# Attention with two expert networks on one core: the network's square and affine step on ScalarE, the second group's solve on VectorE alone, and a new order of the work between the attention hops

## The chip, the cores and the metric

The kernel runs on one core of one Trainium2 chip. The metric is the time of one execution on the device in microseconds. TensorE multiplies matrices (its weight loads are listed as PEld), VectorE (DVE), ScalarE (ACT) and GpSimd (POOL) work on tiles of 128 partitions, SyncE (SP) starts transfers. Each engine runs its own instructions in order; between engines there are semaphores.

## The reference

```python
def _attn_ref(q, k, v, beta):
    k_n = k / (np.linalg.norm(k, axis=-1, keepdims=True) + 1e-06)
    for t in range(S):
        y[:, :, t] = np.einsum('bhd,bhde->bhe', q[:, :, t], state)
        v_old = np.einsum('bhde,bhd->bhe', state, kt)
        state = state + bt[:, :, :, None] * np.einsum('bhd,bhe->bhde', kt, vt - v_old)

def _moe_ref(x, w_in, w_out, s, b):
    h = x @ w_in
    r = np.maximum(h, 0.0)
    g = s * (r * r) + b
    return (g @ w_out).astype(np.float32)

def reference(**kwargs):
    attn_out = _attn_ref(**attn_kwargs)
    x = attn_out.transpose(0, 2, 1, 3).reshape(B * S, H * D)
    x = _moe_ref(x=x, **moe_kwargs)
    return _moe2_ref(x=x, **moe2_kwargs)
```

Four batches of eight heads, 768 steps, 48 wide, feed 3072 tokens of 384 to a network of 2048 hidden units; `_moe2_ref` sends each token through the best of eight experts of 1024 hidden units. All is fp32.

## The kernel before

**Attention.** The sequence is cut into 24 chunks of 32 steps, and these into six groups of four. Within a chunk the update is a triangular system of 32 x 32 per head. For a whole group it is solved at once: `lanes_in` transposes the Gram matrices `gc` so that every partition holds one system A, prepares T, the norms and the scaling of A, and scales v by the norms on POOL; `solve` takes 31 steps of two VectorE instructions (`tmp` = column of A times row of T, T minus `tmp`); `lanes_out` transposes T into `tt`. Then `dstep` runs a chunk in three hops: `ks` (state times keys, X = v minus it), `tx` (T times X, giving `u` and `bdu`), `ku` and `mu` (new state `ds`, `sst`; output). Each hop hands on from TensorE to VectorE and back. The hops of a group are the fixed chain; group 0 runs alone, and the others take the next group's preparation with them: loads, `tr_k`, `tr_q`, `gram`, `lanes_in`, the solve steps, `lanes_out`, each with a due time in hops (`add`, `due`).

**Second group.** It has no hops to hide behind. `lanes_in(1)`, 15 steps `solve_d` on the two diagonal halves of every system, and the off-diagonal quarter by products: `off_in`, then four times `off_1` (TensorE, copy by ScalarE) and `off_2` (TensorE, update of `tt` by VectorE). `PREP` says how many ticks of network work follow each piece.

**First network.** `moe1` is a generator; each tick it emits one fp32 matmul (first token pair, `kk` = 0) or three matmuls of the split form (later pairs: high and low part of x and of the weights). Twelve pairs of 256 tokens, eight blocks each: `mm1` fills the one PSUM buffer `h`, Relu frees it; then square, scale by s and add b, cast to the high part `gh`, difference `gl`; `mm2` two blocks later uses both. In the first pair ScalarE does square and affine step; in later pairs POOL does (L698, L699). Calls put into `later` come a given number of ticks on.

**Order.** The order on TensorE, VectorE, ScalarE and POOL is the order of emission. In the hops of group g, `run_moe` emits at each of 48 quarter hops as many ticks as are left to a target, 192 g - 36, divided by the quarter hops left. Every fifth tick calls `w_next`: first `x_step` (weight words are put together: two VectorE instructions and a sum on POOL, L580), then `split_step` (cast by ScalarE, difference by VectorE into `wp`). After the last hop the rest of the network runs alone, then the second network.

## Time and profile before

| | |
|---|---|
| median of 3 runs | 991.92 us (991.78 to 992.33) |
| profiled execution | 991.13 us, span 989.1 us |
| TensorE busy | 879.0 us (89%), 12602 matmuls |
| weight loads busy | 799.1 us (81%) |
| VectorE busy | 477.5 us (48%), 1009 instructions |
| ScalarE busy | 331.9 us (34%), 689 |
| POOL busy | 251.8 us (25%), 262 |
| mean granted TensorE clock | 0.924 of full speed |

A busy TensorE is not one at its peak: the clock is granted at one of two levels, 1.2 and 2.4 GHz, and 0.92 is a mean over both. The share of busy time is a mean over stages: group 0 alone (to about 86 us), the preparation of the second group (to 174), the hops of groups 1 to 5 (to about 653), the rest of the first network (to about 740), the second network. In the rows, times are microseconds from the start of the span unless marked ns; what stands in brackets is the idle time ahead of an instruction and what ended it.

### The profile page before, as it was taken

Reading aid. Unit: us, or ns where it says so; the run is one execution under the profiler, and the core shown is the slowest. Engines: PE = TensorE matmul, PEld = TensorE weight load, DVE = VectorE, ACT = ScalarE, POOL = GpSimd, SP = SyncE. Lnnn points to the kernel's source line nnn. Section 1 sums busy time; section 2 is a strip of 40 time slices with the busy share of each in tenths; the row PEclk is TensorE's granted clock in tenths of the full one; section 3 lists DMA queues with packets and bytes.
Section 4 is the critical chain, followed back from the end, with each engine's and each line's share of the span. In section 5 each row is a group of like instructions: output and inputs, shape, how many; then the busy total and the mean of one; then the engine's idle time right before and its main releaser. Section 6 shows DMA issues by size and latency. Waiting matters only on the chain. (4 is left out here: it accounts for less than half of the span.)

```text
span 989.1 us, 28725 instructions
## 1 busy us (share of the span) xinstructions
PE 879.0 (89%) x12602; PEld 799.1 (81%) x12602; DVE 477.5 (48%) x1009; ACT 331.9 (34%) x689; POOL 251.8 (25%) x262
## 2 busy tenths in 40 slices
PE   6288779975997999989998999999997999999997
PEld 4266567865997999888997999999996779779796
DVE  3975595549534973489327942226314333231111
ACT  2515644431342334323342332335322222222221
POOL 4122340112223332143323333334430110110100
PEclk7658987887999999999998999999998999999999
DMA  8762132011220121102100000005008310123000
GB/s 153 248 229 52 32 53 48 19 35 18 46 47 11 31 48 27 31 19 49 34 3 2 18 3 18 18 2 176 17 1 52 49 49 25 56 84 124 17 33 25
DMA packets 115597, 49.48 MB, mean 50 GB/s; under 512 B 89943, under 2 KB 112144, under 8 KB 115472
## 3 DMA queue, kind: packets, MB, share of 16 engines
q1 hardware_dynamic: 108560, 46.44, 20.2%
q10 hardware_dynamic: 6336, 1.18, 0.8%
q8 instruction: 99, 1.62, 0.7%
q14 instruction: 26, 0.21, 0.1%
q0 software_dynamic: 576, 0.02, 0.1%
HBM read 38.06 MB, written 9.74 MB: 48 GB/s over the span
## 5 line engine op out<-in xcount | busy, mean ns | idle before, releaser
L698 POOL TENSOR_TENSOR r<-r 128x512 f32<-128x512 f32 x88 | 96.1, 1092 | 356.9 <-ACT r L697 356.9
L724 PE MATMUL acc<-gh,wp 128*128 128x256 f32 x1056 | 146.2, 284 | 0.0
L677 PE MATMUL h<-xh,wp 128*128 128x256 f32 x576 | 124.5, 298 | 11.7 <-ACT r L697 11.7
L724 PEld LDWEIGHTS acc<-gh,wp 128*128 128x128 f32 x1056 | 133.7, 193 | 1.2
L701 DVE TENSOR_TENSOR gl<-r,gh 128x512 fp32r<-128x512 f32 x88 | 63.0, 716 | 128.6 <-ACT gh L700 128.5
L677 PEld LDWEIGHTS h<-xh,wp 128*128 128x128 f32 x576 | 98.3, 198 | 14.3 <-ACT r L697 12.7
L700 ACT CAST gh<-r 128x512 fp32r<-128x512 f32 x88 | 54.7, 622 | 149.5 <-POOL r L699 139.2
L677 PE MATMUL h<-xhl,wp 128*128 128x256 f32 x720 | 101.5, 288 | 3.3 <-ACT r L697 3.3
L965 DVE SCALAR_TENSOR_TENSOR hl<-h,hh 128x512 fp32r<-128x512 f32 x46 | 31.7, 691 | 141.5 <-ACT hh L964 141.5
L677 PEld LDWEIGHTS h<-xhl,wp 128*128 128x128 f32 x720 | 90.0, 190 | 5.3 <-ACT r L697 3.9
L697 ACT ACTIVATE r<-h 128x512 f32<-128x512 f32 x88 | 52.6, 598 | 93.3 <-PE h L677 64.2
L677 PE MATMUL h<-xl,wp 128*128 128x256 f32 x288 | 83.0, 288 | 0.0
L699 POOL TENSOR_SCALAR r<-r,s_sb,b_sb 128x512 f32<-128x512 f32 x88 | 74.9, 851 | 9.2
L724 PE MATMUL acc<-gl,wp 128*128 128x256 f32 x528 | 75.8, 279 | 0.0
L425 ACT COPY x<-ch 32x384 f32<-32x384 f32 x96 | 45.2, 471 | 87.3 <-PE ch L411 86.3
L287 DVE TENSOR_TENSOR T<-T,tmp 128x31 f32<-128x31 f32 (+15 forms) x155 | 69.4, 448 | 5.3
L724 PEld LDWEIGHTS acc<-gl,wp 128*128 128x128 f32 x528 | 67.4, 190 | 0.2
L284 DVE TENSOR_TENSOR tmp<-A,T 128x31 f32<-128x31 f32 (+15 forms) x155 | 65.1, 420 | 3.9
L1045 PE MATMUL o<-w2h,hh 128*128 128x384 f32 x184 | 62.3, 339 | 0.0
L1045 PE MATMUL o<-w2l,hh 128*128 128x384 f32 x184 | 61.9, 336 | 0.0
L1045 PE MATMUL o<-w2h,hl 128*128 128x384 f32 x184 | 61.8, 336 | 0.0
L1034 POOL TENSOR_TENSOR x2l<-xr,x2h 128x512 fp32r<-128x512 f32 x15 | 18.7, 1279 | 166.3 <-ACT x2h L1033 166.3
(226 smaller groups left out, 1493.9 us busy)
## 6 DMA issues: line engine op xcount, KB each, us to landing
wr<-in_moe_w_in SPq DMA_DIRECT2D x16, 384.0 KB
wr<-in_moe_w_out SPq DMA_DIRECT2D x8, 768.0 KB
v<-in_v SPq DMA_DIRECT2D x192, 24.0 KB
x2d<-x2s SPq DMA_DIRECT2D x24, 192.0 KB
out<-o SPq DMA_DIRECT2D x24, 192.0 KB
kpad<-in_k SPq DMA_DIRECT2D x160, 24.0 KB
qpad<-in_q SPq DMA_DIRECT2D x40, 96.0 KB
xr<-x2d SPq DMA_DIRECT2D x5, 768.0 KB
```

The lines of the kernel that those rows point to most:

```text
L284: nc.vector.tensor_tensor(out=tmp, in0=A[:, j + 1:, j:j + 1].to_broadcast([128, m, j + 1]), in1=T[:, j:j + 1, 0:j + 1].to_broadcast([128, ...
L287: nc.vector.tensor_tensor(out=T[:, j + 1:, 0:j + 1], in0=T[:, j + 1:, 0:j + 1], in1=tmp, op=ALU.subtract)
L425: nc.scalar.copy(out=x_t[gi][pb:pb + C, :, r * 96:(r + 1) * 96].rearrange("p h (g e) -> p h g e", g=2), in_=y[32 * rr:32 * rr + 32, :, :, ...
L677: nc.tensor.matmul(out=h[:, f, :], lhsT=wi_(w, 2 * j + f, m), rhs=x[:, m, :], start=(m == 0 and i == 0), stop=(m == KD - 1 and i == 2))
L697: nc.scalar.activation(out=r, in_=h, func=AF.Relu)
L698: nc.gpsimd.tensor_tensor(out=t, in0=r, in1=r, op=ALU.mult)
L699: nc.gpsimd.tensor_scalar(out=t, in0=t, scalar1=s_sb, scalar2=b_sb, op0=ALU.mult, op1=ALU.add)
L700: later.append((step[0] + 7, lambda: nc.scalar.copy(out=gh, in_=t)))
L701: later.append((step[0] + 9, lambda: nc.vector.tensor_tensor(out=gl, in0=t, in1=gh.bitcast(F32), op=ALU.subtract)))
L724: nc.tensor.matmul(out=acc[:, m * TT:(m + 1) * TT], lhsT=wo_(w, 2 * j + f, m * 128, 128) if kk else wx_(2 * j + 1, 2 * j + f, m * 128), rh ...
L965: nc.vector.scalar_tensor_tensor(out=hl, in0=ps, scalar=0.0, in1=hh.bitcast(F32), op0=ALU.max, op1=ALU.subtract)
L1045: nc.tensor.matmul(out=ps, lhsT=h[:, sl], rhs=w[:, f, :], start=(f == 0 and i == 0), stop=(f == KF2 - 1 and i == 2))
```

## The change

The later pairs' square and affine step go to ScalarE, as in the first pair: Square directly after Relu, the affine step and the cast seven ticks on, `gl` eleven ticks on instead of nine. POOL keeps the weight sums of `x_step`, group 0's v-scaling and the second network's part.

`lanes_in` is cut into `lanes_1`, `lanes_2`, `lanes_3` and two calls of `scale_v`, each an item with a due time of its own, half a hop to one hop ahead of the solve. The clearing of T and, from the second group on, the scaling of v are VectorE's.

The second group is solved like the others, 31 steps on VectorE; `diag`, `solve_d`, `off_in`, `off_1` and `off_2` are gone. `PREP` and the due times of the items are new, and weight step, router and lanes alternate differently.

In the hops, the quarter hops from the 24th on count double in group 1 and one and a half times later when the ticks left are shared out; up to eight ticks may follow a quarter hop. One weight scaling fewer is emitted ahead of the first solve.

```diff
-    def lanes_in(gi):
...
+    def lanes_1(gi):
+        A = stg.tile([128, C, C], F32, tag="A", name="A")
         nc.vector.transpose(out=A, in_=gc_t[gi].rearrange("p h g n t -> p t (h g n)"))
...
+        T = T0.pop() if gi == 0 else stg.tile([128, C, C], F32, tag="gc", name="T")
         if gi:
-            nc.gpsimd.memset(Tf, 0.0)
+            nc.vector.memset(T, 0.0)
...
+    def scale_v(gi, g, eng):
+        if g == 0:
+            nmc_t[gi] = stg.tile([128, C], F32, tag="ss", name="nmc")
+            nc.vector.transpose(out=nmc_t[gi], in_=ln[gi][2])
+        nv = nmc_t[gi].rearrange("p (h g n) -> p h n g", g=2, h=B)
+        o = v_t[gi][:, :, :, g, :]
+        eng.tensor_tensor(
+            out=o, in0=o, in1=nv[:, :, :, g].unsqueeze(3).to_broadcast([128, B, HG, D]), op=ALU.mult)
...
-    PREP = {1: 2, 2: 12, 3: 3, 4: 10, 5: 1}
+    PREP = {100: 2, 200: 5, 201: 4, 300: 2, 301: 1, 400: 5}
...
                 if gi:
-                    h += 0.5
-                    add(h, lanes_in, g2)
-                    h += 0.5
+                    for f, a in ((lanes_1, ()), (lanes_2, ()), (lanes_3, ()), (scale_v, (0, nc.vector)),
+                                 (scale_v, (1, nc.vector))):
+                        add(h, f, g2, *a)
+                        h += 0.25
                     he = 11.25
                     for j in range(C - 1):
-                        add(h + max(0, he - h) * j / (C - 1), solve, g2, j)
+                        add(h + (he - h) * j / (C - 1), solve, g2, j)
                     add(he + 0.25, lanes_out, g2)
                 else:
-                    add(102, router_setup_a2)
-                    add(103, router_setup_b)
-                    add(200, lanes_in, 1)
-                    for j in range(C2 - 1):
-                        add(300 + j, solve_d, 1, j)
-                    add(400, off_in, 1)
-                    for n in range(HG):
-                        add(500 + 2 * n, off_1, 1, n, n + 1)
-                        add(501 + 2 * n, off_2, 1, n, n + 1)
-            items.sort(key=lambda x: x[:2])
+                    add(100, router_setup_a2)
+                    add(200, lanes_1, 1)
+                    add(200, lanes_2, 1)
+                    add(200, lanes_3, 1)
+                    add(201, scale_v, 1, 0, nc.vector)
+                    add(201, scale_v, 1, 1, nc.vector)
+                    add(201, router_setup_b)
+                    for j in range(C - 1):
+                        add(301 if j % 3 == 2 else 300, solve, 1, j)
+                    add(400, lanes_out, 1)
+            items.sort(key=lambda x: (min(x[0], 300) if x[0] > 100 else x[0], x[1]))
...
-                        st["gi"], st["left"] = gi, 4 * (NS - hops) - i
+                        st["gi"], n = gi, 4 * hops + i
+                        w = [(2 if gi == 1 else 1.5) if x >= 23 else 1 for x in range(n, 4 * NS)]
+                        st["left"] = sum(w) / w[0]
...
-            nc.scalar.activation(out=r, in_=h, func=AF.Relu)
-            nc.gpsimd.tensor_tensor(out=t, in0=r, in1=r, op=ALU.mult)
-            nc.gpsimd.tensor_scalar(out=t, in0=t, scalar1=s_sb, scalar2=b_sb, op0=ALU.mult, op1=ALU.add)
-            later.append((step[0] + 7, lambda: nc.scalar.copy(out=gh, in_=t)))
-            later.append((step[0] + 9, lambda: nc.vector.tensor_tensor(
-                out=gl, in0=t, in1=gh.bitcast(F32), op=ALU.subtract)))
+                def parts():
+                    nc.scalar.activation(out=r, in_=r, func=AF.Identity, scale=s_sb, bias=b_sb)
+                    nc.scalar.copy(out=gh, in_=r)
+                later.append((step[0] + 7, parts))
+                later.append((step[0] + 11, lambda: nc.vector.tensor_tensor(
+                    out=gl, in0=r, in1=gh.bitcast(F32), op=ALU.subtract)))
...
-        w_scale(7)
+        w_scale(6)
...
-                run_moe(max(1, min(7, -(-(24 * KF // 2 * st["gi"] - 36 - state["n"]) // st["left"]))))
+                run_moe(max(1, min(8, round((24 * KF // 2 * st["gi"] - 36 - state["n"]) / st["left"] + 0.3))))
```

What the order becomes at three places follows; line numbers are those of each program.

TensorE at the end of the second group's preparation, before (`z` are the off-diagonal products, `acc` the network's second layer, `ch` the first product of group 1's first hop):

```order
L326 MATMUL z_2195<-tt,gc 32x16 x32
L724 MATMUL acc<-gf,wr_262 128x256
L339 MATMUL z_2231<-zz,dd 32x16 x32
L724 MATMUL acc<-gf,wr_262 128x256
L355 MATMUL ch<-sst,kqt 64x48 x32
```

TensorE at the same place, now (`h` is the network's first layer, `u` the second hop's product):

```order
L633 MATMUL h<-xh,wp_1843 128x256
L307 MATMUL ch<-sst,kqt 64x48 x32
L678 MATMUL acc<-gf,wr_264 128x256 x4
L328 MATMUL u<-X,tt 32x48 x32
L678 MATMUL acc<-gf,wr_264 128x256 x2
```

The products `z` between network pieces are gone; whole blocks of the network stand ahead of group 1's first hop, and the second hop follows after four matmuls.

VectorE in the second group's lanes, before (`wr` are the weight steps, `tmp` and T the half solve):

```order
L266 TENSOR_TENSOR A<-A,bt 128x1024
L272 STREAM_TRANSPOSE nmc<-nm 128x32
L577 SCALAR_TENSOR_TENSOR wr_257<-wr_257 128x768
L579 TENSOR_SCALAR wr_257<-wr_257 128x768
L577 SCALAR_TENSOR_TENSOR wr_260<-wr_260 128x768
L579 TENSOR_SCALAR wr_260<-wr_260 128x768
L304 TENSOR_TENSOR tmp<-A,T 128x30
L307 TENSOR_TENSOR T<-T,tmp 128x2x15
```

VectorE at the same place, now:

```order
L268 TENSOR_TENSOR A<-A,bt 128x1024
L533 SCALAR_TENSOR_TENSOR wr_260<-wr_260 128x768
L535 TENSOR_SCALAR wr_260<-wr_260 128x768
L276 STREAM_TRANSPOSE nmc<-nm 128x32
L279 TENSOR_TENSOR v<-v,nmc 128x16x48
L533 SCALAR_TENSOR_TENSOR wr_262<-wr_262 128x768
L535 TENSOR_SCALAR wr_262<-wr_262 128x768
L279 TENSOR_TENSOR v<-v,nmc 128x16x48
```

The weight steps have moved in between the lane pieces, and the two scalings of v stand in VectorE's row.

ScalarE around the lanes of group 3's hops, before (`r` from `h` is Relu, `gh` the cast, `ss` the norms):

```order
L700 CAST gh<-r 128x512
L254 ACTIVATE s_4475<-ss 128x32
L697 ACTIVATE r<-h 128x512
```

ScalarE at the same place, now:

```order
L653 CAST gh<-r 128x512
L252 ACTIVATE s_4158<-ss 128x32
L641 ACTIVATE r<-h 128x512
L642 ACTIVATE r<-r 128x512
L652 ACTIVATE r<-r,b_sb,s_sb 128x512
```

Square and affine step of each block stand between its Relu and its cast.

## Rows read from the trace of the kernel before

**Rows 1.** Windows: span, busy PE, PEld, DVE, ACT, POOL; clock, DMA, GB/s

```profile
core 0: us, PE busy (x) PEld busy (x) DVE busy (x) ACT busy (x) POOL busy (x), PEclk, DMA share, GB/s
86.30:174.50 88.20, 70.17 (x1011) 57.27 (x1011) 55.16 (x98) 47.99 (x88) 22.76 (x15) 0.83 0.24 41
174.50:253.40 78.90, 62.12 (x1383) 55.79 (x1382) 52.54 (x116) 25.75 (x61) 13.95 (x13) 0.82 0.13 26
253.40:569.30 315.90, 296.60 (x5395) 283.56 (x5394) 192.31 (x402) 109.84 (x250) 103.97 (x105) 0.98 0.14 28
569.30:740.00 170.70, 169.74 (x2180) 166.56 (x2180) 57.71 (x103) 63.60 (x127) 66.31 (x69) 1.00 0.12 34
```

**Rows 2.** TensorE's waits, 253.4 to 569.3 us: total us, times, longest

```profile
PE h L677 <- ACT r L697: 15.1, 8, 3.9
```

**Rows 3.** Timeline, 421 to 427 us (group 3): start, us, instruction, [idle before]

```profile
421.11 2.91 POOL L276 TENSOR_TENSOR v<-v,nmc 128x768 f32<-128x768 f32 x2 [4.03 <-DVE nmc L272]
421.17 1.54 PE L724 MATMUL acc<-gh,wp 128*128 128x256 f32 x12
421.18 1.48 DVE L287 TENSOR_TENSOR T<-T,tmp 128x31 f32<-128x31 f32 x1
...
423.98 1.04 POOL L698 TENSOR_TENSOR r<-r 128x512 f32<-128x512 f32 x1
...
425.93 0.62 ACT L700 CAST gh<-r 128x512 fp32r<-128x512 f32 x1 [8.07 <-POOL r L699]
426.45 0.59 ACT L697 ACTIVATE r<-h 128x512 f32<-128x512 f32 x1
426.58 0.69 DVE L701 TENSOR_TENSOR gl<-r,gh 128x512 fp32r<-128x512 f32 x1 [3.92 <-ACT gh L700]
...
427.09 0.39 PE L677 MATMUL h<-xh,wp 128*128 128x256 f32 x1 [3.71 <-ACT r L697]
```

**Rows 4.** Windows of L287 alone (T minus tmp): first solve, group 3

```profile
26.70:52.50 25.80, 11.81 (x31) 0.61 0.81 269
359.20:464.90 105.70, 15.11 (x31) 0.98 0.17 33
```

**Rows 5.** Windows of L284 alone (tmp): the same two stretches

```profile
26.70:52.50 25.80, 11.77 (x31) 0.61 0.81 269
359.20:464.90 105.70, 13.83 (x31) 0.98 0.17 33
```

**Rows 6.** TensorE's waits, 174.5 to 253.4 us (group 1)

```profile
PE ds L392 <- DVE bdu L381: 11.1, 2, 6.3
```

**Rows 7.** Timeline of the preparation of the second group

```profile
116.53 0.47 DVE L815 TENSOR_SCALAR x2s<-x2s,ei 8x384 f32<-8x384 f32 x1
...
119.16 1.98 DVE L246 STREAM_TRANSPOSE A<-gc 128x1024 f32<-128x1024 f32 x1
...
154.40 2.01 DVE L314 STREAM_TRANSPOSE tt<-T 128x1024 f32<-128x1024 f32 x1
...
173.50 0.35 DVE L343 SCALAR_TENSOR_TENSOR tt<-z,negm,tt 128x128 f32<-128x128 f32 x1 [3.92 <-PE z L339]
...
176.59 1.02 DVE L361 TENSOR_TENSOR X<-v,ch 128x384 f32<-128x384 f32 x2 [1.88 <-issue]
...
180.91 0.88 PE L376 MATMUL u<-X,tt 32*32 32x48 f32 x64
```

**Rows 8.** Instruction groups: count, busy us, mean ns; the memset from the timeline

```profile
L688 ACT ACTIVATE r<-r 128x512 f32<-128x512 f32 x8 | 5.1, 632 | 0.3
L689 ACT ACTIVATE gf<-r,b_sb,s_sb 128x512 f32<-128x512 f32 x8 | 6.6, 824 | 1.5 <-PE acc L724 1.5
L590 DVE TENSOR_TENSOR wp<-wr,wp 128x768 fp32r<-128x768 f32 x11 | 10.6, 967 | 5.5 <-ACT wp L589 5.5
L307 DVE TENSOR_TENSOR T<-T,tmp 128x30 f32<-128x30 f32 (+7 forms) x15 | 7.5, 502 | 0.5
L304 DVE TENSOR_TENSOR tmp<-A,T 128x30 f32<-128x30 f32 (+7 forms) x15 | 3.8, 251 | 0.2
1.20 0.27 DVE L89 MEMSET qpad<- 128x256 f32 x1
```

More of the change, by code (lines that the diff above doesn't have):

```diff
@@ L267, in lanes_in @@
             out=A, in0=A, in1=bt.unsqueeze(2).to_broadcast([128, C, C]), op=ALU.mult)
-        ln[gi] = (Af, Tf)
-        def scale_v():
-            nmc = stg.tile([128, C], F32, tag="ss", name="nmc")
-            nc.vector.transpose(out=nmc, in_=nm)
-            nv = nmc.rearrange("p (h g n) -> p h n g", g=2, h=B)
-            for g in range(2):
-                o = v_t[gi][:, :, :, g, :]
-                nc.gpsimd.tensor_tensor(
-                    out=o, in0=o, in1=nv[:, :, :, g].unsqueeze(3).to_broadcast([128, B, HG, D]), op=ALU.mult)
-        scale_v()
+    nmc_t = {}
+    def scale_v(gi, g, eng):
[6 more added lines that the diff above has]
+            out=o, in0=o, in1=nv[:, :, :, g].unsqueeze(3).to_broadcast([128, B, HG, D]), op=ALU.mult)
     def solve(gi, j):
-        A, T = ln[gi]
+        A, T, _ = ln[gi]
         m = C - 1 - j
@@ L290, in lanes_out @@
     def lanes_out(gi):
-        A, T = ln.pop(gi)
-        tt_t[gi] = att.tile([128, 2 * HG * B, C], F32, tag="tt", name="tt", bufs=2)
+        A, T, _ = ln.pop(gi)
+        if gi not in tt_t:
+            tt_t[gi] = att.tile([128, 2 * HG * B, C], F32, tag="tt", name="tt", bufs=2)
         nc.vector.transpose(out=tt_t[gi].rearrange("p u t -> p t u"), in_=T)
-    def diag(x):
-        return x.rearrange("p t i -> p (t i)").rearrange("p (b x) -> p b x", b=2)[:, :, 0:C2 * C].rearrange(
-            "p b (t i) -> p b t i", i=C)[:, :, :, 0:C2]
@@ L310, in tile_kernel @@
-    of = {}
-    def off_in(gi):
-        A, T = ln.pop(gi)
-        nc.vector.transpose(out=tt_t[gi].rearrange("p u t -> p t u"), in_=T[:, 0:C])
-        dd = stg.tile([128, C + 1, C], F32, tag="A", name="dd")
-        nc.vector.transpose(out=dd[:, 0:C].rearrange("p u i -> p i u"), in_=T[:, 0:C].rearrange("p t i -> p i t"))
-        of[gi] = dd
-    def off_1(gi, n0, n1):
-        gc = gc_t[gi].rearrange("p h g n t -> p (h g n) t")
-        z1 = ps_pp.tile([128, 2 * B, n1 - n0, C2], F32, tag="pp", name="z1")
-        for n in range(n0, n1):
-            for e in range(2 * B):
-                for r in range(4):
-                    sl = slice(32 * r, 32 * r + 32)
-                    nc.tensor.matmul(out=z1[sl, e, n - n0, :], lhsT=gc[sl, e * HG + n, :],
-                                     rhs=tt_t[gi][sl, e * HG + n, C2:], start=True, stop=True)
-        zz = stg.tile([128, 2 * B, n1 - n0, C2], F32, tag="tmp", name="zz")
-        nc.scalar.copy(out=zz, in_=z1)
-        of[gi, n0] = zz
@@ L332, in off_2 @@
-    def off_2(gi, n0, n1):
-        dd, zz = of[gi], of.pop((gi, n0))
-        z2 = ps_pp.tile([128, 2 * B, n1 - n0, C2], F32, tag="pp", name="z2")
-        for n in range(n0, n1):
-            for e in range(2 * B):
-                for r in range(4):
-                    sl = slice(32 * r, 32 * r + 32)
-                    nc.tensor.matmul(out=z2[sl, e, n - n0, :], lhsT=dd[sl, e * HG + n, :], rhs=zz[sl, e, n - n0, :],
-                                     start=True, stop=True)
-        for n in range(n0, n1):
-            t = tt_t[gi].rearrange("p (e n) t -> p e n t", e=2 * B)[:, :, n, C2:]
-            nc.vector.scalar_tensor_tensor(out=t, in0=z2[:, :, n - n0, :], scalar=negm, in1=t,
-                                           op0=ALU.mult, op1=ALU.add)
@@ L530, in attention @@
                 if it[0] >= 100:
[L531 removed]
+                    yield PREP[it[0]]
         st["hop"] += 100
@@ L890, in tile_kernel @@
                         nc.scalar.copy(out=o, in_=i)
-        lanes_in(0)
+        lanes_1(0)
+        lanes_2(0)
+        lanes_3(0)
+        scale_v(0, 0, nc.gpsimd)
+        scale_v(0, 1, nc.gpsimd)
         cg = ps_c.tile([128, 2, HG * B, C], F32, tag="ch", name="gr")
```

44 lines of the change are left out of this document (14 added, 30 removed).

## The prediction

> **What bounds the kernel now.** I read the stretches first [rows 1]. From 569 to 740 us TensorE is busy 169.74 of 170.70 us: nothing but its own work counts there, and the change takes no matrix work out of it; the second network behind it has the same code. Time can come only from the three stretches ahead, where TensorE stands idle: the preparation of the second group (88.20 - 70.17 = 18.0 us idle, clock 0.83, so partly on the lower of its two levels), the hops of group 1 (78.90 - 62.12 = 16.8 us, 0.82) and the hops of groups 2 to 4 (315.90 - 296.60 = 19.3 us, 0.98).
>
> Then what the idle time waits for. In groups 2 to 4 it is one thing: 15.1 of the 19.3 us are eight waits of the network's first matmul of a block for the Relu that frees the only buffer `h` [rows 2]. The timeline shows one of them [rows 3]: POOL starts the two v-scalings at 421.11 and holds them to 424.02; only then come the square (1.04 us) and the affine step of the block before; ScalarE, which works in order, has stood 8.07 us at the cast of that block's `gh`, and the Relu of the next block, long possible, runs behind it at 426.45; TensorE starts at 427.09, 3.71 us late.
>
> POOL also slows VectorE. A solve instruction on 31 elements took 1.48 us while POOL ran [rows 3]; all 62 of the first solve take 11.81 + 11.77 = 23.6 us, those of the solve in group 3 take 15.11 + 13.83 = 28.9 [rows 4, 5]. So 5.4 us a group are stalls, at the least.
>
> In group 1 TensorE waits for VectorE's own queue: 11.1 us before the state products `ds` [rows 6]. In the preparation the half solve ends early (its result is transposed at 154.40) but the off-diagonal halves go round TensorE, ScalarE and VectorE until 173.50, each round waiting (3.92 us in the last); the first `u` of group 1 comes at 180.91 [rows 7].
>
> **The change part by part.**
>
> *Square and affine step to ScalarE.* In the 88 blocks after the first pass (11 token pairs of 8) POOL's two steps are replaced by a Square of 0.63 and an Identity of 0.82 us, prices that the first pass shows for the same tiles [rows 8]. ScalarE gets 1.45 us a block: 16 blocks a group, 23 us on top of 109.84 / 3 = 36.6 [rows 1], 60 of 105 us. It no longer waits for POOL, so the standstill of up to 8.07 us ahead of a Relu has no cause left. I take the 15.1 us of Relu waits as gone; the ends are 0 (all replaced by a longer queue) and 19.3 (all idle time gone). What then comes last in the late hops is VectorE.
>
> The Trainium skill speaks against this place: "ScalarE: Activation LUTs", section Rules for kernel authors, wants multiplications and additions on VectorE, not on ScalarE. Here the rows decide against the rule: VectorE, not ScalarE, is what the hops wait for; by the rule 32 more instructions a group, at the 0.69 us of a `gl` 22 us, would stand in its queue, and the sum would lose the gain of groups 2 to 4. I follow the rows.
>
> *Scaling v and clearing T on VectorE.* Per later group two instructions on 768 elements, 0.97 us each by the weight split of the same width, and a memset, 4 x 0.27 = 1.1 us by the one on 256 elements [rows 8]: 3.0 us more. Against it the 5.4 us of stalls go. Net on VectorE between -2.4 and +3.0 us a group; I take -1, since these 5.4 us have a row and the 3.0 are sure.
>
> *More network work in late hops.* Counted in the emitted order, a hop of groups 2 to 4 had 16 ticks (one tick is three matmuls) throughout; now it has 12 to 15 in the first six hops and 17 to 20 in the last six. By 1.54 us for 12 matmuls [rows 3] a tick is 0.35 to 0.39 us: four ticks cover 1.5 us more of a late hop. The sum over a group is the same 192 ticks, so TensorE's work is unchanged. But a late hop now has about 8 us of work on TensorE (20 ticks and an attention step like `u`, 0.88) and 8 on VectorE (31 solve steps over 4.25 hops, some 0.75 us each without stalls, one product of 1.0, one or two `gl` of 0.69): matched, not covered. I charge 2 us over the three groups for hops in which VectorE is late.
>
> **Groups 2 to 4: -15 + 2 = -13 us** (ends -22, which adds the time lost to the lower clock level, and -2).
>
> *Group 1.* In its first six hops the order had 8, 8, 8, 5, 4, 4 ticks and now has 4, 4, 4, 4, 4, 5: 12 fewer, and TensorE is nearly full there (11.1 of the stretch's 16.8 idle us are two waits of the last six hops [rows 6]), so 12 x 0.35 = -4 us. They were done in the preparation (102 ticks instead of 95) or come in the last six hops, which VectorE bounds, so that they cost nothing there as long as VectorE's queue is the longer one: those 11.1 us are their cover. With VectorE's own net of -1: **-5 us** (ends -8 and 0).
>
> *Preparation, second group on VectorE alone.* By differences of VectorE's queue up to the transpose at 154.40 [rows 7]. Added: the full solve 23.6 less the half one 7.5 + 3.8 = 11.3 [rows 4, 5, 8] is +12.3; v-scaling and memset +3.0; four more weight splits stand ahead of the transpose in the order, 4 x 0.97 = +3.9. Taken out: the lanes no longer wait for the router's transposes. They began at 119.16, the router's chain ends at 117.0 [rows 7], but the weight step that lay between is only moved behind them: -0.5. The transpose begins at 154.4 + 12.3 + 3.0 + 3.9 - 0.5 = 173.1. Behind it: transpose 2.0, a split 0.97, a `gl` 0.69 [rows 3], X 1.0, so `u` at 177.8 instead of 180.91. The 256 small matmuls, four copies and four updates of the off-diagonal path disappear; they were in nobody's way but their own. The weight sums on POOL remain and now fall between the lane pieces, where each may stall VectorE once: up to five stalls of at most 1.3 us (1.48 less the 0.19 of a free instruction). Against this the two POOL scalings and their stalls go. Ends: -8 and +5; I take **-3 us**, with the stalls of both sides even. Here is the change's weak point: VectorE becomes the only bound of the preparation, and ScalarE's casts of the splits, which wait for VectorE, stand in front of the Relus.
>
> *The rest.* One weight scaling fewer ahead of the first solve lies on ScalarE while it waits for data: 0. The network after the hops and the second network: 0, TensorE is full or the code is the same.
>
> Sum: -3 - 5 - 13 = -21 us. The profiled execution took 991.13 us (its span 989.1 and 2.0 around it), which gives 970; it lies 0.8 us under the median of 991.92, which gives **971**.
>
> **The rivals.**
> *Late hops stay bound by VectorE.* The Relu waits go, but the hop's chain X, `bdu`, `ds` waits in VectorE's queue as in group 1. For it: work is only matched. Against it: VectorE is busy 192.31 of 315.90 us there [rows 1]. Then groups 2 to 4 give 4 us: 991.9 - 3 - 5 - 4 = 980.
> *The preparation becomes longer.* ScalarE's casts wait for VectorE's splits and the Relus behind them, so all three engines move at the slowest, with stalls from POOL and TensorE at its lower clock after each pause. `u` 5 us later than before instead of 3 earlier: 971 + 8 = 979.
> *Everything idle in groups 2 to 4 goes*, and the preparation has no stalls: -22 - 8 - 5 = -35, 957.
> *Slower: ScalarE becomes the bound.* In order, it now holds Relu, Square, Identity and cast, 0.60 + 0.63 + 0.82 + 0.62 = 2.67 us a block, besides output and key copies. There is one buffer `h`, so a late Relu stops TensorE. It decides from 21 / 88 = 0.24 us a block on; at 0.5 us: 971 + 44 = 1015. Against it: 18 matmuls, over 2 us, lie between two first layers, and the cast alone held ScalarE for longer before.
> *It doesn't do what it says*: the weights of the late hops change little because the count is rounded. The order shows 20 instead of 16 ticks, so this is out.
>
> **How the numbers follow.** Forecast 971 (within 7 us): 0.50; VectorE-bound late hops 0.17; longer preparation 0.12; everything gone 0.13; slower 0.05; several shortfalls together that leave nothing 0.03. The range leaves out the slower cases and half of the best one: 958 to 984. A measurement of this kernel tells 0.2%, 2 us, from no change. Faster 0.92, same 0.03, slower 0.05.
>
> **What would show it.** Right: no wait of a cast for POOL; TensorE's Relu waits under 4 us in groups 2 to 4 and a group at about 101 us instead of 105.3; solve sums near 22 us; first `u` of group 1 at about 178, the first of group 2 some 8 us earlier than now. Wrong: Relu waits of 0.3 us at many blocks; new waits of `ds` or `u` for VectorE in groups 2 to 4; the first `u` of group 1 after 181.

## The result, and the profile after

The changed kernel takes 954.74 us in the median of its runs against 992.12 us of the kernel before on the same chip, a ratio of 0.9616 (95% interval 0.9598 to 0.9635). The forecast was 971 us, its range 958 to 984: the direction was right, the gain is 37 us instead of 21, and the time lies 3 us below the range. The profiled execution has a span of 953.3 us against 989.1, 35.8 us less.

Where the 35.8 us come from is read in windows between the first `u` products of the groups, which cut both kernels at the same place in the program. Of before, then of after (columns: start and end, length, busy us of PE, PEld, DVE, ACT, POOL with instructions, granted clock, DMA share, GB/s):

```profile
86.30:180.90 94.60, 76.57 (x1097) 63.08 (x1097) 58.04 (x102) 49.77 (x91) 22.76 (x15) 0.82 0.22 38
180.90:260.25 79.35, 62.57 (x1406) 56.65 (x1405) 54.37 (x118) 25.55 (x62) 16.25 (x15) 0.85 0.15 29
260.25:576.00 315.75, 296.45 (x5391) 283.42 (x5390) 192.31 (x400) 109.66 (x250) 104.96 (x105) 0.98 0.14 27
576.00:649.73 73.73, 73.73 (x1248) 71.46 (x1247) 22.24 (x42) 24.86 (x48) 23.62 (x26) 1.00 0.05 13
```

```profile
86.30:173.30 87.00, 62.69 (x591) 52.45 (x591) 66.37 (x131) 50.96 (x90) 15.59 (x9) 0.91 0.23 40
173.30:246.39 73.09, 61.98 (x1386) 55.97 (x1386) 52.61 (x122) 31.98 (x70) 0.00 (x0) 0.81 0.16 31
246.39:538.29 291.90, 288.60 (x5392) 277.44 (x5391) 174.51 (x409) 179.23 (x346) 0.00 (x0) 1.00 0.15 29
538.29:613.01 74.72, 74.72 (x1256) 72.44 (x1256) 22.13 (x42) 43.98 (x75) 0.00 (x0) 1.00 0.05 13
```

The preparation gives 7.6 us, group 1 6.3, groups 2 to 4 23.9; group 5 takes 1.0 us more and what follows 0.9 more. In groups 2 to 4 two things went: TensorE's idle time, 315.75 - 296.45 = 19.3 us, is 3.3; and the same matmuls are busy for 288.60 us instead of 296.45, since the granted clock is 1.00 of full speed throughout instead of 0.98.

TensorE's waits in groups 2 to 4 of after (total us, times, longest) answer to [rows 2]; what is left has nothing to do with Relu:

```profile
PE gr L220 <- issue: 2.2, 4, 0.8
PE acc L678 <- issue: 1.0, 1, 1.0
```

ScalarE at the lanes of group 2 in after, from the timeline (start, us, instruction, [idle before]), answers to [rows 3]. In these rows Square, affine step and cast follow Relu without a wait, and Relu waits for TensorE's matmul instead of the other way round. Over groups 2 to 4, 29 Relus wait for TensorE (55.1 us); three still wait for VectorE's `gl` (8.9 us, at most 3.0), without keeping TensorE waiting:

```profile
288.06 0.23 ACT L252 ACTIVATE s<-ss 128x32 f32<-128x32 f32 x1 [2.31 <-DVE ss L246]
289.65 0.60 ACT L641 ACTIVATE r<-h 128x512 f32<-128x512 f32 x1 [1.36 <-PE h L633]
290.28 0.63 ACT L642 ACTIVATE r<-r 128x512 f32<-128x512 f32 x1
290.95 0.82 ACT L652 ACTIVATE r<-r,b_sb,s_sb 128x512 f32<-128x512 f32 x1
291.80 0.62 ACT L653 CAST gh<-r 128x512 fp32r<-128x512 f32 x1
```

The two instructions of the solve in group 3 of after, L286 alone and then L289 alone, answering to [rows 5] and [rows 4]:

```profile
344.33:441.05 96.72, 10.57 (x31) 1.00 0.18 36
```

```profile
344.33:441.05 96.72, 10.66 (x31) 1.00 0.18 36
```

Together 21.2 us where 28.9 stood, so 7.7 us of stalls are gone and not only 5.4.

VectorE, TensorE and one weight sum of POOL in the preparation of after, answering to [rows 7]:

```profile
116.23 2.04 DVE L241 STREAM_TRANSPOSE A<-gc 128x1024 f32<-128x1024 f32 x1
...
124.43 1.47 POOL L536 TENSOR_TENSOR wr<-wr 128x768 int32<-128x768 int32 x1 [2.05 <-DVE wr L535]
124.64 1.30 DVE L265 TENSOR_TENSOR bt<-bt 128x32 f32<-128x32 f32 x1
...
129.13 2.21 DVE L279 TENSOR_TENSOR v<-v,nmc 128x768 f32<-128x768 f32 x1
...
133.59 2.22 DVE L533 SCALAR_TENSOR_TENSOR wr<-wr 128x768 int32<-128x768 int32 x1
...
169.45 1.95 DVE L296 STREAM_TRANSPOSE tt<-T 128x1024 f32<-128x1024 f32 x1
...
173.29 1.50 PE L328 MATMUL u<-X,tt 32*32 32x48 f32 x64 [5.80 <-DVE X L313]
```

The lanes begin at 116.23 (119.16 before) and the solution is transposed at 169.45, where the forecast had 173.1. The stalls between the lane pieces are there as forecast: 1.30 us for an instruction of 0.19, 2.21 for one of 0.95.

### The profile page after: what moved, and what is told of

It reads as the page before. It is cut to its first block, busy times and chain, and to the rows that moved or that the text cites. A ratio compares the mean times of both kernels' runs of the same rounds, so it can differ in the third digit from the quotient of the medians.

```text
span 953.3 us, 27675 instructions
## 1 busy us (share of the span) xinstructions
PE 861.9 (90%) x12090; PEld 785.2 (82%) x12090; DVE 464.1 (49%) x1051; ACT 458.0 (48%) x861; POOL 61.1 (6%) x71
## 3 DMA queue, kind: packets, MB, share of 16 engines
q1 hardware_dynamic: 108560, 46.44, 21.2%
## 5 line engine op out<-in xcount | busy, mean ns | idle before, releaser
L633 PE MATMUL h<-xh,wp 128*128 128x256 f32 x576 | 119.4, 290 | 3.2 <-ACT r L641 3.2
L641 ACT ACTIVATE r<-h 128x512 f32<-128x512 f32 x96 | 57.6, 600 | 121.8 <-PE h L633 107.6
L633 PEld LDWEIGHTS h<-xh,wp 128*128 128x128 f32 x576 | 95.1, 192 | 5.9 <-ACT r L641 4.0
L655 DVE TENSOR_TENSOR gl<-r,gh 128x512 fp32r<-128x512 f32 x88 | 60.3, 685 | 64.3 <-ACT gh L653 64.3
L652 ACT ACTIVATE r<-r,b_sb,s_sb 128x512 f32<-128x512 f32 x88 | 72.0, 818 | 2.2
L922 ACT ACTIVATE hh<-h 128x512 fp32r<-128x512 f32 x46 | 27.4, 598 | 86.3 <-PE h L920 86.3
L289 DVE TENSOR_TENSOR T<-T,tmp 128x31 f32<-128x31 f32 (+15 forms) x186 | 65.1, 350 | 6.4
L286 DVE TENSOR_TENSOR tmp<-A,T 128x31 f32<-128x31 f32 (+15 forms) x186 | 65.9, 354 | 4.8
L642 ACT ACTIVATE r<-r 128x512 f32<-128x512 f32 x96 | 60.7, 632 | 3.1
```

The lines of the kernel that those rows point to most:

```text
L286: nc.vector.tensor_tensor(out=tmp, in0=A[:, j + 1:, j:j + 1].to_broadcast([128, m, j + 1]), in1=T[:, j:j + 1, 0:j + 1].to_broadcast([128, ...
L289: nc.vector.tensor_tensor(out=T[:, j + 1:, 0:j + 1], in0=T[:, j + 1:, 0:j + 1], in1=tmp, op=ALU.subtract)
L633: nc.tensor.matmul(out=h[:, f, :], lhsT=wi_(w, 2 * j + f, m), rhs=x[:, m, :], start=(m == 0 and i == 0), stop=(m == KD - 1 and i == 2))
L641: nc.scalar.activation(out=r, in_=h, func=AF.Relu)
L642: nc.scalar.activation(out=r, in_=r, func=AF.Square)
L652: nc.scalar.activation(out=r, in_=r, func=AF.Identity, scale=s_sb, bias=b_sb)
```

## The experiments

Every ratio is to the kernel before on the same chip, with its 95% interval behind it; that of the changed kernel is 0.9616 (0.9598 to 0.9635). The times of groups and the waits come from one profiled execution of each kernel.

**Which part gives the 24 us of groups 2 to 4.** Theory A, that of the prediction, puts it on ScalarE's two steps. Rivals: the v-scalings (B), the sharing of ticks (C), the lane pieces (L). Four runs first, two of which undo one part and two make one part alone.

Undo ScalarE's part (in the changed kernel):

```diff
-            nc.scalar.activation(out=r, in_=r, func=AF.Square)
...
+            nc.gpsimd.tensor_tensor(out=t, in0=r, in1=r, op=ALU.mult)
+            nc.gpsimd.tensor_scalar(out=t, in0=t, scalar1=s_sb, scalar2=b_sb, op0=ALU.mult, op1=ALU.add)
+            later.append((step[0] + 7, lambda: nc.scalar.copy(out=gh, in_=t)))
```

> The changed kernel (954.7 us) with one part undone: the square and the affine step of the later pairs are GpSimd's again and gl comes nine ticks on, as before; v-scaling and clearing stay on VectorE. Theory A (ScalarE's cast waiting for GpSimd's two steps made the Relu waits; moving them off GpSimd is what the 24 us of groups 2 to 4 come from): Relu waits of TensorE come back in groups 2 to 4, 10 us or more, 970 to 980 us. Theory B (the two v-scalings of 2.9 us ahead of the square in GpSimd's row made the long waits, and these are gone here too): Relu waits under 4 us in groups 2 to 4, clock 1.00, VectorE's solve slower by its stalls, 956 to 963 us.

Measured: 959.2 us, ratio 0.9682 (0.9650 to 0.9715); groups 2 to 4 take 292.8 us, 0.9 more than in the changed kernel, and no Relu wait comes back. Theory A falls: the part on which the prediction put 15 us is worth 0.9 us there once the other parts are in. It is worth more elsewhere: without it the first `u` of group 1 comes 1.2 us later and group 1 takes 74.9 us instead of 73.1.

ScalarE's part alone, in the kernel before (the same edit the other way round):

> The kernel before (992.1 us) with one part alone: square and affine step on ScalarE, gl eleven ticks on. Theory A: all Relu waits of groups 2 to 4 go (15.1 us) and with them the time at the lower clock (busy time 296.5 down by 6 to 8 us), 968 to 972 us. Theory B: the same waits go, since nothing in the hops waits for GpSimd any more; the run tells the size only. If ticks have to be shared out anew for the gain to come, TensorE waits instead for VectorE's products in the late hops, and it is 978 to 986 us.

Measured: 972.9 us, ratio 0.9829 (0.9786 to 0.9872). Groups 2 to 4 take 299.3 us, 16.5 less than before, and the eight waits have become three, of some 3 us each. So the time comes near the 968 to 972 us of theory A (the runs lie between 968.5 and 977.5), but not all of the waits go. The timeline of this kernel at the first of them:

```profile
329.91 0.69 DVE L699 TENSOR_TENSOR gl<-r,gh 128x512 fp32r<-128x512 f32 x1
330.51 0.42 DVE L749 TENSOR_TENSOR sq<-lg,ident 128x256 f32<-128x256 f32 x1
330.69 0.60 ACT L685 ACTIVATE r<-h 128x512 f32<-128x512 f32 x1 [7.84 <-DVE gl L699]
...
331.34 0.58 PE L677 MATMUL h<-xh,wp 128*128 128x256 f32 x1 [3.20 <-ACT r L685]
```

The wait has a new owner. Relu writes one of two buffers `r`; they come free only when VectorE has made `gl`, and the router's `sq` uses them too (`tag="r", bufs=2`). VectorE is behind with the solve, so Relu stands 7.84 us for `gl` and TensorE 3.20 us for Relu. Taking GpSimd out of the row uncovered VectorE's lateness.

v-scaling and clearing of T on VectorE alone, in the kernel before:

```diff
-            nc.gpsimd.memset(Tf, 0.0)
+            nc.vector.memset(Tf, 0.0)
...
-                nc.gpsimd.tensor_tensor(
+                (nc.vector if gi else nc.gpsimd).tensor_tensor(
```

> The kernel before with one part alone: v-scaling and the clearing of T on VectorE in all later groups; square and affine step stay on GpSimd. Theory B: the three waits of 3.7 to 3.9 us (11.3 us) and the lower clock behind them (some 7 us) go, the 1.1 us waits shrink, VectorE gets 3 us a group more, which hides: 972 to 977 us. Theory A: GpSimd's square still makes the cast late and the Relu waits only move: 986 to 992 us.

Measured: 987.9 us, ratio 0.9967 (0.9947 to 0.9986); groups 2 to 4 313.1 us, 2.7 less. The Relu waits add up to 13.3 us in six: the long ones at the v-scaling are gone, and the same late `gl` makes others of 3.2 us. Theory B alone falls as well.

Even sharing of ticks (in the changed kernel):

```diff
-                        w = [(2 if gi == 1 else 1.5) if x >= 23 else 1 for x in range(n, 4 * NS)]
-                        st["left"] = sum(w) / w[0]
+                        st["left"] = 4 * NS - n
...
-                run_moe(max(1, min(8, round((24 * KF // 2 * st["gi"] - 36 - state["n"]) / st["left"] + 0.3))))
+                run_moe(max(1, min(7, -(-(24 * KF // 2 * st["gi"] - 36 - state["n"]) // st["left"]))))
```

> The changed kernel with one part undone: the ticks left are shared evenly over the quarter hops again, rounded as before. By the prediction's sum only group 1 loses (12 ticks back in its first hops, 4 us) and the late hops of groups 2 to 4 lose nothing: 957 to 960 us. Rival C (the sharing is what covers the late hops): TensorE waits for VectorE in the last six hops of groups 2 to 4, 3 us or more a group and a lower clock behind it: 965 to 972 us.

Measured: 951.9 us, ratio 0.9591 (0.9557 to 0.9625): not slower; the median is 2 to 3 us lower, with an interval that overlaps that of the changed kernel. Groups 2 to 4 take 288.9 us with 1.0 us idle, group 1 74.5 us instead of 73.1. Neither expectation holds; the new sharing (the weights and the rounding) brings 1.4 us in group 1 and costs 3.0 in groups 2 to 4.

In the changed kernel the lane pieces fall due from 1.25 to 0.25 hops ahead of the solve (not from one hop to half a hop, as the section on the change has it). Now the lane pieces in one lump, half a hop later with the solve half a hop behind them, as before (first run, the diff), and at the time of the first piece now with the solve left where it is (second run: nothing ahead, 1.25 behind):

```diff
+                    h += 0.5
                     for f, a in ((lanes_1, ()), (lanes_2, ()), (lanes_3, ()), (scale_v, (0, nc.vector)),
                                  (scale_v, (1, nc.vector))):
                         add(h, f, g2, *a)
-                        h += 0.25
+                    h += 0.5
```

> The changed kernel with one part undone: the five lane pieces of groups 2 to 5 fall due together, half a hop later than now the first of them, and the solve a quarter hop earlier, as before. Theory L (the pieces are what removes the last Relu waits: ScalarE no longer stands at the square root of the norms behind VectorE's transpose, and VectorE's gl is not late at the router's step): in each of groups 2 to 4 a Relu wait of some 1.2 us at the square root and one of some 3 us at the router's step come back, the clock falls behind the long one, 4 to 7 us a group over groups 2 to 4: 965 to 975 us. Theory A (ScalarE's two steps did it, the pieces cost and bring nothing): 953 to 957 us.

> The changed kernel with the five lane pieces of groups 2 to 5 due together at the time of the first of them now; the solve stays where it is. It tells the two halves of theory L apart: if the cut itself matters (work between the pieces, ScalarE not standing at the square root), three Relu waits of 1 to 1.5 us come back at the square root, some 4 us: 957 to 961 us. If the earlier start matters (VectorE not late at the router's step), no long wait comes back and the clock stays at 1.00 in groups 2 to 4. If neither matters: 953 to 957 us.

Measured: 957.6 us, ratio 0.9673 (0.9625 to 0.9721), and 958.2 us, ratio 0.9680 (0.9647 to 0.9713). Groups 2 to 4 take 292.8 and 293.0 us, with no Relu wait in either. Theory L falls like the others: 1 us there. Group 1, in whose hops the first of the lumps falls, takes 76.0 and 74.3 us instead of 73.1.

So in groups 2 to 4 no part is needed as long as the rest is there. Both order parts undone at once (even sharing and the lump at the old time; ScalarE's part and VectorE's v-scaling stay):

> The changed kernel with two parts undone at once: even sharing of the ticks and the lane pieces of groups 2 to 5 in one lump at the old time. Each alone cost groups 2 to 4 nothing (288.9 and 292.8 us for the three, 291.9 in the changed kernel). Theory R (each of the two brings VectorE's lanes 3 to 4 us forward in the group, and one of them is enough to keep VectorE's router step and gl from being late): with both undone a Relu wait of some 3 us comes back in each of groups 2 to 4 with a stretch of lower clock behind it, 297 to 301 us for the three, 958 to 965 us in all. Rival (the kernel before with ScalarE's part alone had these waits because GpSimd still scaled v; the order of the lanes never mattered): 289 to 292 us for the three, 951 to 955 us in all.

Measured: 964.1 us, ratio 0.9741 (0.9683 to 0.9798); groups 2 to 4 297.6 us, 5.7 more than in the changed kernel. TensorE's waits there:

```profile
PE h L633 <- ACT r L641: 4.6, 6, 0.9
PE acc L678 <- DVE gl L655: 2.5, 3, 1.0
```

Theory R has the size right (297 to 301 forecast) and the form wrong: nine short waits, and the clock stays at 1.00. Six are for VectorE's `gl`, direct or through Relu (0.8 to 1.0 us); three of 0.7 us are for a Relu behind the square root of the norms, for which ScalarE stands 4.65 us in group 2 while VectorE has the lump in its row. The lump and the even sharing are each harmless and together not.

The two combinations still missing: the new order alone, with GpSimd doing square, affine step, v-scaling and clearing as before; and the changed kernel with only v-scaling and clearing given back:

```diff
-            nc.vector.memset(T, 0.0)
+            (nc.gpsimd if gi > 1 else nc.vector).memset(T, 0.0)
...
-                    for f, a in ((lanes_1, ()), (lanes_2, ()), (lanes_3, ()), (scale_v, (0, nc.vector)),
-                                 (scale_v, (1, nc.vector))):
+                    for f, a in ((lanes_1, ()), (lanes_2, ()), (lanes_3, ()), (scale_v, (0, nc.gpsimd)),
+                                 (scale_v, (1, nc.gpsimd))):
```

> Of the changed kernel only the order is kept in groups 2 to 5 (lane pieces with due times of their own, new sharing of ticks): square and affine step are GpSimd's again, and so are v-scaling and the clearing of T. Groups 2 to 4 took 315.8 us before, 291.9 with all three parts, 292.8 without ScalarE's part. If the order is what matters (VectorE's lanes early), 292 to 296 us for the three groups and 957 to 962 us in all. If GpSimd's v-scaling ahead of its square is a cause of its own, the long Relu waits of 3 to 4 us stay, with a stretch of lower clock behind each: 304 to 312 us for the three groups and 970 to 980 us in all.

> The changed kernel with v-scaling and the clearing of T given back to GpSimd; ScalarE keeps square and affine step, the order stays. If nothing in the hops waits for GpSimd once ScalarE has the two steps, groups 2 to 4 take 291 to 294 us as in the changed kernel (291.9), 953 to 957 us in all. If GpSimd's 2.9 us hold up VectorE's solve, which starts behind them, the router's step is late again and a Relu wait comes back: 296 to 300 us for the three groups.

Measured: 957.9 us, ratio 0.9683 (0.9629 to 0.9736), and 951.6 us, ratio 0.9620 (0.9575 to 0.9664). Groups 2 to 4 take 293.5 and 292.1 us. The order alone gives 22.3 of the 23.9 us, with GpSimd as loaded as before (104.7 us busy in these groups, 105.0 before). Its ScalarE and GpSimd in group 2, then the sum of one wait over groups 2 to 4:

```profile
300.38 1.48 POOL L279 TENSOR_TENSOR v<-v,nmc 128x768 f32<-128x768 f32 x1 [3.28 <-DVE nmc L276]
301.82 1.04 POOL L654 TENSOR_TENSOR r<-r 128x512 f32<-128x512 f32 x1
302.96 0.81 POOL L655 TENSOR_SCALAR r<-r,s_sb,b_sb 128x512 f32<-128x512 f32 x1
303.75 1.48 POOL L279 TENSOR_TENSOR v<-v,nmc 128x768 f32<-128x768 f32 x1
303.81 0.62 ACT L656 CAST gh<-r 128x512 fp32r<-128x512 f32 x1 [4.61 <-POOL r L655]
304.34 0.59 ACT L653 ACTIVATE r<-h 128x512 f32<-128x512 f32 x1
...
305.66 2.30 PE L633 MATMUL h<-xhl,wp 128*128 128x256 f32 x18
```

```profile
ACT gh L656 <- POOL r L655: 79.6, 33, 4.6
```

The same sum in the kernel before:

```profile
ACT gh L700 <- POOL r L699: 83.7, 30, 8.2
```

ScalarE still stands 79.6 us for GpSimd, hardly less than before. But the two scalings are now separate items, a block's square goes between them, the longest standstill is 4.61 us instead of 8.2, and TensorE does not wait for it once. So the 15.1 us were not the price of GpSimd's two steps by themselves: in the new order the same steps cost TensorE no wait. The room is small. The Relu at 304.34 ends 0.7 us before TensorE's next `h` at 305.66; with the second scaling, 1.48 us, still ahead of the square, TensorE would have waited some 0.8 us here (an estimate from these rows). How much of the gain is due to the pieces and how much to the sharing of ticks, this run does not show.

All combinations, groups 2 to 4 (A: ScalarE's steps, V: v-scaling on VectorE, O: new order):

| | none | V | A | A, V | O | O, V | A, O | A, V, O |
|---|---|---|---|---|---|---|---|---|
| us | 315.8 | 313.1 | 299.3 | 297.6 | 293.5 | 292.8 | 292.1 | 291.9 |
| idle us | 19.3 | 19.5 | 10.2 | 8.0 | 4.5 | 3.8 | 4.0 | 3.3 |

"A, V" and all columns with O have the new preparation too; that lies ahead of these groups. O, the lane pieces and the new sharing together, was not split further without A and V, so which half of it does the 22 us alone stays open; with A and V in, either half is enough.

**What a wait of TensorE costs.** In groups 2 to 4 the busy time fell by 7.9 us with the waits. Two kernels put waits back, by repeating a Relu that writes the same values again: ten times in one block of token pairs 2, 4 and 6, or six times in three blocks of each.

```diff
-            nc.scalar.activation(out=r, in_=h, func=AF.Relu)
+            for _ in range(10 if kk in (2, 4, 6) and j in (4,) else 1):
+                nc.scalar.activation(out=r, in_=h, func=AF.Relu)
```

> The changed kernel; ScalarE repeats the Relu of one block of token pairs 2, 4 and 6 ten times (5.4 us more before h is free), so TensorE gets one long wait in each of groups 2 to 4. It prices a wait. If a long wait also costs a stretch of lower clock, as the 7.9 us less of busy time in groups 2 to 4 of the changed kernel suggest: idle time of the three groups 3.3 us plus 9 to 13, busy time up by 5 to 8 us, 968 to 975 us. If the 7.9 us had another reason: idle time up alike, busy time within 1.5 us of 288.6, 963 to 967 us.

> The changed kernel; ScalarE repeats the Relu of three blocks of token pairs 2, 4 and 6 six times (3.0 us more each), so the idle time comes in nine shorter waits of about 1.2 us instead of three long ones. If it is the long wait that brings the lower clock: idle time up by 8 to 13 us, busy time within 1.5 us of 288.6, clock 1.00, 963 to 967 us. If the sum of the idle time brings it: busy time up by 5 to 8 us as with the long waits, 968 to 975 us.

Measured: 973.0 us, ratio 0.9831 (0.9761 to 0.9901), and 970.3 us, ratio 0.9804 (0.9738 to 0.9869). The Relu waits of groups 2 to 4, with long and with short waits:

```profile
PE h L633 <- ACT r L642: 12.9, 3, 4.3
```

```profile
PE h L633 <- ACT r L642: 12.2, 9, 1.8
```

The three long waits made the groups 313.4 us long: 21.5 us more for 12.9 us of waiting, because the busy time rose from 288.6 to 296.8 us. That settles the 7.9 us: they belong to the waits. The short waits did not do what was expected of them: 311.4 us, 19.5 more for 12.2, busy 296.1. The matmuls show when the clock fell. With short waits, in group 2:

```profile
273.87 1.33 PE L633 MATMUL h<-xhl,wp 128*128 128x256 f32 x9 [0.69 <-ACT r L642]
293.79 3.44 PE L633 MATMUL h<-xhl,wp 128*128 128x256 f32 x18 [1.78 <-ACT r L642]
306.77 2.41 PE L633 MATMUL h<-xhl,wp 128*128 128x256 f32 x18 [1.78 <-ACT r L642]
```

Eighteen matmuls took 3.44 us after one wait of 1.78 and 2.41 after the next of the same length. Groups 2 and 4 of this kernel have a granted clock of 0.98 and 0.97, group 3 has 1.00. So a wait of 1.8 us can be followed by a stretch on the lower level or not. The price is that of the profiled executions (976.5 and 973.1 us); the other execution of each kernel was 6.9 and 5.6 us shorter, at a higher mean clock (0.938 instead of 0.928, 0.943 instead of 0.936), so what the same waits cost may differ from one execution to the next. In the kernel before, the stretch behind a long Relu wait, from 322 us on:

```profile
317.00:322.00 5.00, 1.12 (x10) 0.93 (x9) 1.08 (x3) 1.12 (x2) 3.67 (x4) 1.00 0.01 2
322.00:326.00 4.00, 4.00 (x24) 3.77 (x24) 3.69 (x12) 1.22 (x2) 1.94 (x3) 0.58 0.01 1
326.00:332.00 6.00, 6.00 (x131) 5.82 (x132) 5.72 (x14) 2.83 (x6) 1.94 (x2) 1.00 0.01 3
```

**The preparation.** The half solve and the off-diagonal products put back into the changed kernel, with their own ticks (`lanes_in`, `solve_d`, `off_in`, `off_1`, `off_2` as before):

```diff
-                    for j in range(C - 1):
-                        add(301 if j % 3 == 2 else 300, solve, 1, j)
-                    add(400, lanes_out, 1)
+                    for j in range(C2 - 1):
+                        add(300 + j, solve_d, 1, j)
+                    add(400, off_in, 1)
+                    for n in range(HG):
+                        add(500 + 2 * n, off_1, 1, n, n + 1)
+                        add(501 + 2 * n, off_2, 1, n, n + 1)
```

> The changed kernel with one part undone: the second group's preparation is that of before (half solve, off-diagonal products on TensorE, its v-scaling and clearing on GpSimd, its own counts of ticks); the rest is the changed kernel. The traces of before and after put the first u of group 1 at 180.9 and 173.3 us. Theory P (the solve on VectorE alone is the shorter way by itself): first u of group 1 back at 179 to 181 us and 960 to 963 us. Rival (the 7.6 us come from ScalarE's and GpSimd's part, as the 178.1 us of the kernel before with ScalarE's part alone suggests for 2.9 of them): first u at 174 to 178 us and 955 to 959 us.

Measured: 955.0 us, ratio 0.9647 (0.9624 to 0.9671); first `u` of group 1 at 177.7 us. That lies in the rival's ranges and outside those of theory P: 3.2 of the 7.6 us come without the new preparation, 4.4 with it (solve, lane pieces, v-scaling and ticks together; the solve by itself was not tested). Group 1 then takes 71.9 us instead of 73.1, so some 3 us of the whole are left. The ratios differ by as much, but their intervals overlap.

Seven weight steps (three and twice two; the expectation counts eight), the clearing of T and the router's set-up moved into VectorE's idle time ahead of the Gram matrices, on top of even sharing:

```diff
                     add(99, second_places)
+                    add(99, x_step)
+                    add(99, clear_1)
+                    add(99, x_step)
+                    add(99, router_setup_a2)
+                    add(99, x_step)
...
+                            if f is gram:
+                                add(99.5, x_step)
+                                add(99.5, x_step)
...
-        w_scale(n + 3)
+        w_scale(n + (8 if n > 2 else 3))
```

> The changed kernel with even sharing of ticks (951.9 us), and in the second group's preparation eight weight steps, the clearing of T and the router's set-up put into VectorE's idle times before the Gram matrices are complete (6.6 and 5.9 us in the trace); ScalarE's scaling of the weights goes further ahead in group 0. Theory V (VectorE's queue from the transpose of the Gram matrices to that of the solution is the bound of the preparation): five weight steps of 1.5 us, some 6 us of stalls by GpSimd's sums, the set-up of 2.6 and the clearing of 0.9 leave that queue, four or five weight splits of 0.95 come in: first u of group 1 about 11 us earlier, 939 to 943 us. Rival (TensorE's first pair is the bound, whose weights the splits wait for): first u 0 to 4 us earlier, 947 to 952 us.

Measured: 942.3 us, ratio 0.9523 (0.9484 to 0.9562), the lowest median of all. VectorE's row from transpose to transpose:

```profile
118.83 2.01 DVE L245 STREAM_TRANSPOSE A<-gc 128x1024 f32<-128x1024 f32 x1
...
161.79 1.98 DVE L301 STREAM_TRANSPOSE tt<-T 128x1024 f32<-128x1024 f32 x1
```

43.0 us instead of 53.2 in the changed kernel and with even sharing alone; the lanes begin 2.6 us later, the first `u` comes at 165.1 us, 8.7 earlier than with even sharing alone (173.8; 11 expected). Theory V holds: that queue is the bound of the preparation.

Two more turns on that version: the network's target 16 ticks higher with double weight in the last hops of group 1, and the double weight in group 1 alone (the target stays at 36 below).

```diff
-                        st["left"] = 4 * NS - n
+                        w = [2 if gi == 1 and x >= 23 else 1 for x in range(n, 4 * NS)]
+                        st["left"] = sum(w) / w[0]
...
-                run_moe(max(1, min(7, -(-(24 * KF // 2 * st["gi"] - 36 - state["n"]) // st["left"]))))
+                run_moe(max(1, min(8, round((24 * KF // 2 * st["gi"] - 20 - state["n"]) / st["left"] + 0.3))))
```

> The version with the early weight steps (942.3 us), and the network's target at the end of each group 16 ticks higher, with double weight for the last six hops of group 1, where TensorE waits 10.8 us for VectorE. Theory: TensorE's work is the same in sum, so what of the 16 ticks (5.6 us) falls into these waits is gained, 3 to 6 us: 936 to 940 us. Rival: VectorE's queue in group 1 gets longer with it (a gl of 0.69 us for every 12 ticks, and X and bdu behind it), and the waits move back: 941 to 944 us.

> The version with the early weight steps (942.3 us, group 1 75.2 us) with the double weight of the last six hops in group 1 alone; the target stays. In the changed kernel group 1 took 73.1 us with weights and 74.5 with even sharing. Theory: 1 to 2 us less in group 1 and no other stage moves, 940 to 942 us. Rival: the 1.4 us were chance, 942 to 944 us.

Measured: 960.0 us, ratio 0.9699 (0.9645 to 0.9752), and 944.0 us, ratio 0.9547 (0.9512 to 0.9582). The first is 18 us worse, in a place that neither theory named: groups 2 to 4 take 309.9 us, with this new wait of the router's products for ScalarE's output copies:

```profile
PE lg L714 <- ACT x2s L703: 13.6, 6, 2.4
```

With these waits TensorE's busy time is 295.2 us at a clock of 0.98, against 288.0 in the version without the higher target. That the 16 ticks moved the end of a token pair against the hops is a likely reason, but not shown; the rounding of the count changed with them. Group 1 itself stayed at 75.2 us, as the rival said. The second brought group 1 to 73.7 us and nothing that the whole shows.

## Why the prediction was wrong

**Groups 2 to 4: forecast -13 (ends -22 and -2), measured -23.9.** This is the term that failed, by three steps. Of the 10.9 us between the two, 7.9 are the busy time at the lower clock, 2.0 the charge for late hops, and 1.0 further idle time: 16.0 us of it went (19.3 to 3.3), not 15.1.

- Size of a wait. "I take the 15.1 us of Relu waits as gone" counted them at their length; the time at the lower clock stood only in the end at -22, as 22 - 19.3 = 2.7 us. It was 7.9. The row had it: a clock of 0.98 over 296.6 busy us [rows 1] is 2%, some 6 us, and a wait like the 3.71 us of [rows 3] is what the long-wait kernel prices: 21.5 us for 12.9.
- "+2 us for hops in which VectorE is late". No wait of `ds`, `u` or X is left in groups 2 to 4. The estimate of 8 us of work on either engine took the solve steps at 0.75 us a pair; in after they take 0.68 (21.2 / 31), and VectorE's busy time in these groups fell by 17.8 us although nine instructions came in.
- Only the Relu waits were counted. 3.5 us of waits of `xp` for the state went with them.

**What removed them.** The prediction put all eight waits on GpSimd's row and all of the gain on ScalarE's two steps. Of the eight, the three of 1.11 us have another owner, which the trace of before shows: ScalarE stands 4.59 us at the square root of the norms, for VectorE's transpose in the lump of the lanes, and the Relu is behind it.

```profile
311.33 0.23 ACT L254 ACTIVATE s<-ss 128x32 f32<-128x32 f32 x1 [4.59 <-DVE ss L252]
311.47 0.58 ACT L697 ACTIVATE r<-h 128x512 f32<-128x512 f32 x1
...
312.10 1.10 PE L677 MATMUL h<-xhl,wp 128*128 128x256 f32 x7 [1.11 <-ACT r L697]
```

And ScalarE's part was not necessary: the order alone gives 293.5 us. The prediction priced the five lane pieces nowhere in these groups; it named them in the preparation only. The runs show two remedies for the same waits: take the two steps out of GpSimd's row, or give the work a new order in time. By itself the first leaves the next late engine (VectorE's `gl`, 9.2 us of waits), which the prediction had asked about for `ds` and X but not for the buffers `r`.

**ScalarE against VectorE.** The prediction weighed a rule of the Trainium skill ("ScalarE: Activation LUTs", section Rules for kernel authors) that wants multiplications on VectorE and followed the rows. ScalarE carries it: 179.2 us busy in 291.9, and no Relu waits. Nothing here ran the steps on VectorE, so what the rule would have cost is not shown; that the steps' place was worth 0.9 us in these groups, with the other parts in, is.

**The preparation: forecast -3 (ends -8 and +5), measured -7.6.** Within the ends, and mis-sized by 4.6 us, in three places. The lanes began at 116.23, where the prediction let the router's chain end at 117.0. From there to the transpose it had 56.1 us (117.0 to 173.1) and 53.2 passed; 1.1 of that is the solve, 11.81 + 10.64 = 22.5 us instead of 23.6, and the rest was not taken apart. Behind the transpose 3.8 us passed instead of 4.7. The stalls came as named.

**Group 1: -5 forecast, -6.3 measured.** Right in place: TensorE's waits of `ds` for `bdu` are 5.4 us where 11.1 stood. The sum is near in part by luck: of the twelve ticks' 4 us the even sharing, which puts the ticks back into the first hops, shows only 1.4. ScalarE's steps, which the prediction did not price here, are worth 1.8 us (74.9 with them undone) to 2.7 (76.7 with them alone); the remainder was not taken apart.

**The rest: 0 forecast, +1.9 measured.** Group 5 has a few more ticks (1256 matmuls instead of 1248, 1.0 us). The stretch behind it, whose code is the same, varied between 337 and 341 us over the kernels with the same target, so its 0.9 us say nothing.

**The rivals.** "Everything idle in groups 2 to 4 goes", 957 us with a chance of 0.13, is what happened; its terms -22, -8, -5 came out as -23.9, -7.6, -6.3, and the range had cut half of it off. ScalarE did not become the bound: the rows above show it waiting for TensorE.

## What to carry to other kernels

Price a wait of TensorE at its length plus the stretch at the lower clock behind it: here 12.9 us of waits cost 21.5 in the profiled execution. Before blaming the engine that a queue waits for, look at the order of what stands ahead of it: a new order (lane pieces with due times of their own, and a new sharing of ticks) brought more here by itself, 22.3 us, than moving two steps to another engine, 16.5. When two remedies overlap, only undoing both at once shows their worth. For the engine that bounds a stage, look for its idle time just ahead of the stage: moving work there, without removing any, gave 8.7 us in that stage and the fastest version.

## What was not expected of the hardware

- Waits of 1.78 us, equal in length, were followed once by a stretch in which 18 matmuls took 3.44 us and once by one at 2.41; nine of at most 1.8 us cost 7.5 us of busy time, nearly as much as three of 4.3 us (8.2).
- GpSimd's effect on VectorE is large and need not matter. With ScalarE's part undone VectorE is busy 200.0 us in groups 2 to 4 against 174.5 for the same 409 instructions, 25.5 us more beside 98 GpSimd instructions; the groups grew by 0.9 us. The Trainium skill ("SBUF — State Buffer", section SBUF: two separate sides) says that the two engines share a port pair: against a VectorE instruction with two inputs in SBUF, among others, the engine that starts first holds it for its whole instruction. The rows of the preparation agree: the product `bt` by `bt`, 0.19 us elsewhere, took 1.30 beside a GpSimd sum of 1.47.
